# Fewer, larger and later loads on SP in a fused linear-attention and feed-forward kernel

## The chip, the core and the metric

The kernel runs on one core of one Trainium2 chip. The metric is the device time of one execution in microseconds. Engines: PE (TensorE, matrix products), PEld (its weight loads), DVE (VectorE), ACT (ScalarE), POOL (GpSimd), and SP, which computes nothing: it issues DMAs, in the order of the program. POOL issues four DMAs too, for a weight. A DMA lands some microseconds after it was issued.

## The reference

Four batches of eight heads, 768 positions, head dimension 64: a recurrence with a decay for each head, then a feed-forward layer with a squared ReLU over the 3072 x 512 result. All inputs and the output are float32.

```python
gamma = 1.0 - 2.0 ** (-5.0 - np.arange(H, dtype=np.float32))
for t in range(S):
    state = gamma * state + einsum('bhd,bhe->bhde', k[:, :, t], v[:, :, t])
    y[:, :, t] = (1 / sqrt(D)) * einsum('bhd,bhde->bhe', q[:, :, t], state)
x = y.transpose(0, 2, 1, 3).reshape(B * S, H * D)      # 3072 x 512
h = np.maximum(x @ w_in, 0.0)                          # w_in 512 x 2048
out = (h * h) @ w_out                                  # w_out 2048 x 512
```

## The kernel before

**Chunks.** The sequence of each batch is cut in 6 chunks of 128 positions, 24 chunks in all (chunk m is chunk m % 6 of batch m // 6). For a chunk the kernel makes scores (q times k, masked), a running state (k times v, summed over the chunks of a batch) and outputs (scores times v, plus state times q). The decay is put into q and into k or v as a factor, so that the state is a plain sum. The outputs of two chunks make a block of 256 rows for the feed-forward layer (the first block has four chunks).

**Chunks 8 to 23** go like this (`attend2`): POOL casts k to bf16 with two heads side by side (`cast_k2`, L658, two instructions); SP transposes the result by DMA (`transpose_k2`, L681, from ks_bdp to kT); DVE scales v (`scale_v2`, L667, one instruction over all heads) and POOL copies it (L675, two instructions); for each second chunk DVE scales q (L366) and SP transposes it by DMA (`dma_transpose_q`, L425). Then PE: the state with the first half of the chunk's positions (`state2`, L724; it reads the cast k and the scaled v), the scores (`scores2`, L697; it reads kT and qT), the state with the second half, the outputs (L746 and L753).

**Chunk 4** is done in an older way: DVE scales k (`scale_k`, L366 into ks), PE transposes it (L412).

**Loads.** q comes in one DMA for two chunks (`load_q`, 512 KB, L105). From chunk 8 on, k and v come through `batch_loads` (L147): one DMA for each head, so 8 DMAs cover `size` chunks; all 8 must land before v of the first of these chunks can be scaled, and 4 of them (the even heads, the odd heads) for each of the two casts of k. `(8, "k")` covers chunks 8 to 11 with size 4, `(12, ...)` chunks 12 to 17 and `(18, ...)` chunks 18 to 23 with size 3, in two rounds each. A row that a DMA moves is 64 numbers, 256 bytes.

**The order is written by hand.** Between any two pieces of the feed-forward work on PE lies a numbered *place*, and `put(place, what, ...)` hangs a step on it; within one place steps go in the order in which they were put. A place is about 0.87 us of PE work from place 49 on (eight products of 128x256). Each engine runs its own instructions in this order and waits where a semaphore says so; SP knows no places as times, so that it runs ahead or falls behind. `attend2` puts the steps of chunk m from its output place d: k cast at d-18, q scaled at d-19 and d-18, q transposed at d-16, k transposed at d-13, v scaled at d-9, first state at d-6, scores at d-5, second state at d-3. For m = 12, d is 86, and 8 places more for each next chunk; chunks 8 to 11 have places of their own (`ahead`). `load_q(m)` is at d-33. The two stores of a block come in the second and third piece of the next block's first product (L886 and L888). For chunk 10: q transposed at 54, k transposed at 57. For chunk 11: v of chunk 10 scaled and k of chunk 11 cast at 60, k transposed at 63.

The first weight, w_in, is loaded and cast in quarters (`cast_w`, "V" on DVE, "G" on POOL); the quarters of w_out are loaded by POOL, the first at place 10. The sums of `seven_products` use seven products where a product of two-by-two blocks has eight; they add work on DVE that PE reads.

Of the kernel before, what the change touches and what calls it, by code (L numbers as in the profile page):

```python
# [28 lines left out]
def kernel(  # L29
# [97 lines left out]
    def stage_tile(size):  # L127
        t = stage.tile([P, 2 * NCH * NPAIR * D], FP32, name="stage")
        return t[:, 0:size]
# [3 lines left out]
    def batch_loads(m, name, size):  # L133


        b, i = chunks[m]
        src, to = (k, raw_k) if name == "k" else (v, raw_v)
        t = kept_tiles.pop((m, name), None)
        if t is None:
            t = stage_tile(2 * NCH * NPAIR * D)  # L140
        t = t.rearrange("s (p w d) -> s p w d", p=NPAIR, d=D)
        for j in range(NCH - i):
            to[m + j] = t[:, :, 2 * j : 2 * j + 2].rearrange("s p u d -> s u p d")
        for w in range(0, NCH - i, size):
            for hh, rows in enumerate(halves):
                for p in range(NPAIR):
                    nc.sync.dma_start(  # L147
                        t[rows, p, 2 * w : 2 * (w + size)],
                        src[b, 2 * p + hh, (i + w) * C : (i + w + size) * C].rearrange(
                            "(w s) d -> s w d", s=64  # L150
                        ),
                    )
                    yield
# [1061 lines left out]
    def put(place, what, *args):  # L1215
        parts.setdefault(place, []).append((what, args))
# [4 lines left out]
    def attend(m, q_at, qturn_at, k_at, v_at, turn_at, scores_at, state_at, outputs_at):  # L1221
        if m % 2 == 0:
            for r, place in enumerate(q_at):
                put(place, scale_q, m, r)
            put(qturn_at, transpose_q, m)
        put(k_at, scale_k, m)
        put(v_at, cast_v, m)
        put(turn_at, transpose_k, m, m == 4)
        for half, place in enumerate(scores_at):
            put(place, scores, m, half)  # L1230
        put(state_at, state, m)
        put(outputs_at, outputs, m)
# [16 lines left out]
    put(10, load_w_out, 0)  # L1249
    put(11, cast_w, "in", 3, (0,), ".VGV")  # L1250
    put(12, cast_w, "in", 3, (1,), "GVGV")
    attend(4, (8, 9), 11, 11, 11, 12, (14, 15), 15, 17)
    put(13, load_w_out, 1)
    put(17, load_q, 6)
    attend(5, None, None, 17, 18, 18, (20, 21), 21, 23)
# [44 lines left out]
    for m, d in zip(range(PACK_FROM, NCHUNK), done):  # L1300
# [4 lines left out]
    places = {  # L1305
        (8, "k"): [23, 23, 24, 24, 25, 32, 32, 33],
        (8, "v"): [33, 33, 34, 34, 35, 35, 36, 36],
        (12, "k"): [49, 50, 51, 52, 53, 54, 55, 56] + [74 + j for j in range(8)],
        (12, "v"): [58, 59, 60, 61, 62, 64, 65, 66] + [82 + j for j in range(8)],
        (18, "k"): [92 + 4 * j // 3 for j in range(8)] + [117 + 4 * j // 3 for j in range(8)],  # L1310
        (18, "v"): [103 + 4 * j // 3 for j in range(8)] + [128 + 4 * j // 3 for j in range(8)],
    }
    for (m, name), at_places in places.items():
        loads = batch_loads(m, name, 4 if m == 8 else 3)
        for place in at_places:
            put(place, next, loads)

# [53 lines left out]
```

## Time and profile before

| what | value |
|---|---|
| runs shown | 210.73, 212.37, 212.43 us; median 212.37 |
| profiled execution | 213.31 us, of it a span of 211.1 us |
| granted TensorE clock | 0.989 |
| PE busy | 195.8 us (93%) |
| PEld, DVE, ACT, POOL busy | 165.0, 153.5, 136.0, 69.4 us |
| loads of 96 KB by L147 | 32 for k, 32 for v; median 3.4 and 3.3 us to landing |
| loads of 128 KB by L147 | 8 for k, 8 for v; median 4.9 and 5.7 us to landing |
| DMA transposes of k, of q | 16, median 3.5 us to landing; 8, median 4.8 us |
| stores of 256 KB | 23, median 2.6 us to landing |

The span is the time from the program's first to its last instruction; times of single rows count from its start. In rows in order of time the first number is the start and the second the duration, xN says how many instructions are merged, and the bracket holds the idle time of the engine before it and what ended it. For SP a row's duration is the issue alone, not the transfer. In rows of one source line, the three numbers are the shortest, the median and the longest duration in ns.

### The profile page before, as it was taken

Reading aid. Unit: us, or ns where it says so; the run is one execution under the profiler, and the core shown is the slowest. Engines: PE = TensorE matmul, PEld = TensorE weight load, DVE = VectorE, ACT = ScalarE, POOL = GpSimd, SP = SyncE. Lnnn points to the kernel's source line nnn. Section 1 sums busy time; section 2 is a strip of 40 time slices with the busy share of each in tenths; the row PEclk is TensorE's granted clock in tenths of the full one; section 3 lists DMA queues with packets and bytes.
Section 4 is the critical chain, followed back from the end, with each engine's and each line's share of the span. In section 5 each row is a group of like instructions: output and inputs, shape, how many; then the busy total and the mean of one; then the engine's idle time right before and its main releaser. Section 6 shows DMA issues by size and latency. Waiting matters only on the chain.

```text
span 211.1 us, 5854 instructions
## 1 busy us (share of the span) xinstructions
PE 195.8 (93%) x2369; PEld 165.0 (78%) x2373; DVE 153.5 (73%) x305; ACT 136.0 (64%) x276; POOL 69.4 (33%) x134
## 2 busy tenths in 40 slices
PE   5789979999999999699999699799999999999993
PEld 1467634876988998688989599699989999998883
DVE  4777899498897777489597489389688697564374
ACT  8365876577853677492795495584795785783730
POOL 5332458903130254062236044142244236010000
PEclk9889999999999999999999999999999999999999
DMA  6999999998999969689669889999969750500202
GB/s 170 290 317 383 285 252 237 200 198 199 236 174 186 241 180 218 136 207 235 145 183 216 167 197 214 138 266 162 172 175 233 154 101 13 143 0 0 102 0 99
DMA packets 93258, 38.12 MB, mean 181 GB/s; under 512 B 68528, under 2 KB 89264, under 8 KB 93232
## 3 DMA queue, kind: packets, MB, share of 16 engines
q1 hardware_dynamic: 91120, 35.66, 78.1%
q0 software_dynamic: 2112, 2.10, 6.1%
q8 instruction: 18, 0.29, 0.7%
q14 instruction: 8, 0.07, 0.1%
HBM read 27.26 MB, written 6.29 MB: 159 GB/s over the span
## 4 chain that ended last, share of the span: by engine, by line
PE 69%; DMA 15%; DVE 6%; ACT 4%; issue 3%; POOL 1%; SPq 1%; DVEq 0%
PE psf L803 29%; PE psf L837 12%; PE tp L837 8%; PE psf L1096 6%; DMA kT<-ks_bdp 6%; DMA stage<-in_moe_w_in_dram 4%; DMA w_out_bf<-in_moe_w_out_dram 4%; PE psf L1002 3%; DMA qn<-in_q_dram 2%; PE st L697 2%; PE y L753 1%; PE y L746 1%; PE c_ps L724 1%; DVE h L774 1%; ACT h L812 1%
## 5 line engine op out<-in xcount | busy, mean ns | idle before, releaser
L803 PE MATMUL psf<-xt,w_in_bf 128*128 128x256 bf16 (+2 forms) x878 | 92.1, 259 | 0.1
L803 PEld LDWEIGHTS <-w_in_bf 128*128 128x128 bf16 x880 | 70.9, 98 | 10.6 <-issue 0.4
L812 ACT ACTIVATE h<-psf 128x512 bf16<-128x512 f32 x96 | 56.3, 595 | 23.9 <-PE psf L803 23.4
L774 DVE TENSOR_TENSOR h<-h 128x512 bf16<-128x512 bf16 x72 | 32.8, 472 | 15.3 <-ACT h L812 15.0
L658 POOL CAST ks_bdp<-stage 64x512 bf16<-64x512 f32 x32 | 24.0, 750 | 48.3 <-issue 24.5
L675 POOL COPY v_bd<-v 64x512 bf16<-64x512 bf16 x32 | 20.6, 642 | 40.9 <-DVE v L667 29.2
L837 PEld LDWEIGHTS <-h 128*128 128x128 bf16 x288 | 26.3, 98 | 3.6 <-DVE h L774 0.7
L833 DVE TENSOR_TENSOR osb<-psf,u 128x256 f32<-128x256 f32 x34 | 13.7, 422 | 17.4 <-ACT u L878 10.1
L366 DVE TENSOR_TENSOR qs<-qn,qf 128x512 bf16<-128x512 f32 x22 | 17.4, 795 | 1.0 <-DMA qn<-in_q_dram 1.0
L760 ACT ACTIVATE xt<-y 128x512 bf16<-128x512 f32 x16 | 12.0, 748 | 8.8 <-PE y L753 8.8
L704 DVE TENSOR_TENSOR pt<-st,cmask 128x512 bf16<-128x512 f32 x16 | 11.0, 687 | 6.1 <-PE st L697 5.9
L837 PEld LDWEIGHTS <-k_bd 128*128 128x128 bf16 x144 | 13.8, 98 | 1.6
L772 ACT ACTIVATE h<-h 128x512 bf16<-128x512 bf16 x24 | 14.6, 627 | 0.5
L733 ACT ACTIVATE s_bd<-c_ps 64x256 bf16<-64x256 f32 x29 | 10.6, 366 | 3.4 <-PE c_ps L724 3.3
L667 DVE TENSOR_TENSOR v<-stage,kf 128x512 bf16<-128x512 f32 x16 | 12.6, 786 | 0.0
L837 PE MATMUL tp<-w_out_bf,h 128*128 128x256 bf16 x72 | 11.2, 273 | 0.2 <-DVE h L774 0.2
L734 ACT ACTIVATE s_bd<-c_ps 64x256 bf16<-64x256 f32 x29 | 11.0, 379 | 0.4
L697 PE MATMUL st<-qT,kT 128*128 128x64 bf16 x128 | 6.4, 193 | 5.1 <-DMA kT<-ks_bdp 5.1
L833 DVE TENSOR_TENSOR k_bd<-h 128x512 bf16<-128x512 bf16 x18 | 10.7, 597 | 0.3
L837 PE MATMUL psf<-w_sum,h 128*128 128x256 bf16 x72 | 10.8, 273 | 0.0
L697 PEld LDWEIGHTS <-kT 128*128 128x128 bf16 x128 | 5.6, 98 | 6.1 <-DMA kT<-ks_bdp 5.9
L837 PE MATMUL psf<-w_sum,k_bd 128*128 128x256 bf16 x80 | 10.4, 273 | 0.0
(144 smaller groups left out, 310.1 us busy)
## 6 DMA issues: line engine op xcount, KB each, us to landing
qn<-in_q_dram SPq DMA_DIRECT2D x12, 512.0 KB, 5.6
out_dram<-osb SPq DMA_DIRECT2D x23, 256.0 KB, 2.6
stage<-in_k_dram SPq DMA_DIRECT2D x32, 96.0 KB, 3.4
stage<-in_v_dram SPq DMA_DIRECT2D x32, 96.0 KB, 3.3
stage<-in_moe_w_in_dram SPq DMA_DIRECT2D x4, 512.0 KB, 6.9
stage<-in_moe_w_in_dram SPq DMA_DIRECT2D x2, 1024.0 KB, 10.9
w_out_bf<-in_moe_w_out_dram POOLq DMA_DIRECT2D x4, 512.0 KB, 10.6
kn<-in_k_dram SPq DMA_DIRECT2D x2, 512.0 KB, 6.4
```

Of the source, the lines that this page charges most:

```text
L366: engine.tensor_tensor(out=out, in0=by, in1=table[:, :, None].to_broadcast([P, H, D]), op=ALU.mult)
L658: nc.gpsimd.tensor_copy(ks[rows, :, hh, :].rearrange("s (u p) d -> s u p d", u=2), kn[rows])
L667: nc.vector.tensor_tensor(out=v2.rearrange("s (u p) d -> s u p d", u=2), in0=vn, in1=kf2[:, i, :, :, None].to_broadcast([P, 2, NPAIR, D]), ...
L675: nc.gpsimd.tensor_copy(v_bd[rows, :, hh, :], v2[rows])
L697: nc.tensor.matmul(st[:, c, :], lhsT=kT[:, c, :], rhs=half_of(a["qT"], p, u), start=True, stop=True,)
L772: nc.scalar.activation(hv, hv, AF.Square)
L774: nc.vector.tensor_mul(hv, hv, hv)
L803: nc.tensor.matmul(hp, lhsT=w_in_bf[g][:, cb, fq * 128 : (fq + 1) * 128], rhs=xts[tb][:, cb, cols], start=(cb == 0), stop=(cb == NCB - 1),)
L812: nc.scalar.activation(hv, hp[:], AF.Relu)
L833: nc.vector.tensor_tensor(out=out, in0=in0, in1=in1, op=op)
L837: nc.tensor.matmul(to, lhsT=left[:, j], rhs=right(j) if callable(right) else right[:, j], start=(start and j == 0), stop=(stop and j == NF ...
L1096: nc.tensor.matmul(to[:], lhsT=left(j), rhs=right(j), start=(start and j == 0), stop=(j == NFB // 2 - 1), skip_group_check=True,)
```

## The change

- Chunk 4's k is scaled on DVE at place 10, not 11: ahead of the weight casts of place 11.
- Batch 12's first round (chunks 12 to 14): the k loads go from places 49 to 56 to places 58 to 65, the v loads from 58 to 66 to places 66 to 73. So they come after chunk 10's transposes (54 and 57) in SP's order; five k loads stand ahead of chunk 11's k transpose (63), all but the last v load ahead of chunk 12's (73). Before, all eight k loads stood ahead of chunk 10's k transpose and 13 of the 16 ahead of chunk 11's.
- Batch 18 (chunks 18 to 23): one round of 8 loads of 192 KB for k and one for v, where there were two rounds of 8 loads of 96 KB for each. k at places 94, 96, ... 108 (before: 92 to 101, and 117 to 126), v at 109, 111, ... 123 (before: 103 to 112, and 128 to 137). The v of chunk 18 is scaled at place 125; its k is transposed at 121.

The bytes that are moved, the rows of 256 bytes and the arithmetic stay as they are.

```diff
-    attend(4, (8, 9), 11, 11, 11, 12, (14, 15), 15, 17)
+    attend(4, (8, 9), 11, 10, 11, 12, (14, 15), 15, 17)
...
-        (12, "k"): [49, 50, 51, 52, 53, 54, 55, 56] + [74 + j for j in range(8)],
-        (12, "v"): [58, 59, 60, 61, 62, 64, 65, 66] + [82 + j for j in range(8)],
-        (18, "k"): [92 + 4 * j // 3 for j in range(8)] + [117 + 4 * j // 3 for j in range(8)],
-        (18, "v"): [103 + 4 * j // 3 for j in range(8)] + [128 + 4 * j // 3 for j in range(8)],
+        (12, "k"): [58 + j for j in range(8)] + [74 + j for j in range(8)],
+        (12, "v"): [66 + j for j in range(8)] + [82 + j for j in range(8)],
+        (18, "k"): [94 + 2 * j for j in range(8)],
+        (18, "v"): [109 + 2 * j for j in range(8)],
     }
     for (m, name), at_places in places.items():
-        loads = batch_loads(m, name, 4 if m == 8 else 3)
+        loads = batch_loads(m, name, {8: 4, 12: 3, 18: 6}[m])
         for place in at_places:
             put(place, next, loads)
```

## The prediction

> **What bounds the kernel now.** I read the page first: PE 93% busy, and the chain of waits gives 6% to DMA kT<-ks_bdp. The rows in order of time for PE then show where it stands still, apart from the start:
>
> ```profile
> 86.16 0.41 PE L697 MATMUL st<-qT,kT 128*128 128x64 bf16 x8 [1.86 <-DMA kT<-ks_bdp]
> 118.33 0.41 PE L697 MATMUL st<-qT,kT 128*128 128x64 bf16 x8 [1.73 <-DMA kT<-ks_bdp]
> 134.95 0.41 PE L697 MATMUL st<-qT,kT 128*128 128x64 bf16 x8 [1.47 <-DMA kT<-ks_bdp]
> ```
>
> These are the scores of chunks 10, 14 and 16, each waiting for its k transposed by DMA: 5.06 us in all. From 135 to 205 us the windows show PE busy for 5.00 of every 5 us, so only what comes earlier can move the end. Why the transposes are late is in the rows of SP and of POOL:
>
> ```profile
> 80.50 2.03 SPq L147 DMA_DIRECT2D stage<-in_k_dram  x3
> 82.64 1.27 SPq L681 DMA_TRANSPOSE kT<-ks_bdp  x1
> 83.96 3.30 SPq L147 DMA_DIRECT2D stage<-in_v_dram  x5
> 87.36 2.37 SPq L681 DMA_TRANSPOSE kT<-ks_bdp  x1
> ...
> 93.45 2.22 SPq L425 DMA_TRANSPOSE qT<-qs  x1
> 95.78 1.38 SPq L681 DMA_TRANSPOSE kT<-ks_bdp  x1
> 97.20 5.58 SPq L147 DMA_DIRECT2D stage<-in_k_dram  x7
> ```
> ```profile
> 76.16 1.36 POOL L658 CAST ks_bdp<-stage 64x512 bf16<-64x512 f32 x2
> 82.05 1.28 POOL L675 COPY v_bd<-v 64x512 bf16<-64x512 bf16 x2 [4.53 <-PE psf L837]
> 83.39 1.28 POOL L658 CAST ks_bdp<-stage 64x512 bf16<-64x512 f32 x2
> ```
>
> Chunk 10's k was cast at 77.52, its transpose issued at 82.64: SP issues one DMA right behind another and is late by its own work. A load of 96 KB takes it 0.62 us and 0.05 to the next (the five from 83.96 to 87.36: 0.68 each); I use 0.67.
>
> **Part 1, chunk 4's k scaled a place sooner.** DVE does ks (0.68 us) ahead of two squares and two weight casts. PE's wait for it goes:
>
> ```profile
> 31.47 0.40 PE L412 MATMUL tp<-ident,ks 128*128 128x128 bf16 x4 [1.09 <-DVE ks L366]
> ...
> 36.34 1.04 PE L1002 MATMUL psf<-w_out_bf,h 128*128 128x512 bf16 x4 [0.35 <-DMA w_out_bf<-in_moe_w_out_dram]
> ```
>
> But the next wait is fixed: w_out lands at 36.30, issued by POOL at 28.69 after a cast that waited for w_in, none of it touched. The 1.09 us move into that wait. The casts end 0.7 later, near 31.5, where the products that read them began at 31.70. Value 0; were w_out not the cover, it would be -1.1, and +0.7 if PE caught the casts.
>
> **Part 2, batch 12's first loads behind chunk 10's transposes.** Between 70.81 and chunk 10's k transpose SP keeps four stores (some 2.1 us), a q load (0.45 to 1.90) and chunk 10's q transpose (1.38 to 2.68): done by 77.5 at the latest, as the cast ends. It issues at 77.6 and lands 3.47 later (as before) at 81.1; PE wants it at 86.16 - 1.86 = 84.30. **-1.86**, with 3.2 us to spare.
>
> What is late next: the loads were moved, not removed. SP issues five (78.9 to 82.3), then meets chunk 11's transpose, which must wait for POOL's second cast, 83.39 + 1.28 = 84.67. That cast stands behind the v_bd copies of 82.05, which wait for DVE's v and not for SP. So SP, with nothing to spare, waits 2.0 us at chunk 10's and 2.4 us at chunk 11's, and the loads behind it wait too. Chunk 11's transpose goes at 84.73, 2.63 sooner than before, but eight loads that were ahead of it (8 x 0.67 = 5.36) are now behind. Before, the stretch from its issue to the end of chunk 12's transpose took 97.20 - 87.36 = 9.84 us; now seven more loads lie in that: 9.84 + 4.69 = 14.53, and the eighth v load of batch 12 goes out at 99.26 (before: 91.10). At the page's 3.3 us it lands at 102.6. All eight are needed by one DVE operation, and PE needs its result:
>
> ```profile
> 98.88 0.69 DVE L667 TENSOR_TENSOR v<-stage,kf 128x512 bf16<-128x512 f32 x1
> ```
> ```profile
> 100.59 0.28 PE L724 MATMUL c_ps<-v,ks_bdp 128*128 128x64 bf16 x4
> ```
>
> Chunk 12's v is scaled from 102.6 to 103.3. PE, 1.86 early, would be at chunk 12's state (L724) at 98.73 and stands for **+4.6**. Queued behind the waiting operation on DVE: three adds to osb and chunk 12's mask; PE is held by the same load, so they cost nothing more. Bounds by the rows: landing 2.5 to 5.1 us, and issues of 0.9 us a q or k transpose less where the queue has drained: +1.7 to +6.4. I take the middle because the before run spent its 9.84 us on these very DMAs. Net at chunk 12: +2.7.
>
> Chunk 14: its transpose (issued at 114.88) came 27.52 us after chunk 11's; now 84.73 + 27.52 + 5.36 = 117.61, landing 3.41 later at 121.0. PE arrives at 118.33 - 1.73 + 2.7 = 119.3 and waits 1.7 where it waited 1.73: **0.0**.
>
> **Part 3, the last batch in eight issues a tensor in place of sixteen.** 192 KB in one issue is not in the trace. The nearest rows are one line's issues of 128 KB (49 to 64 us) and of 96 KB (later):
>
> ```profile
> L147 SPq DMA_DIRECT2D stage<-in_v_dram x8: 595/672/1675, 56.5 to 62.7; - x8
> ```
> ```profile
> L147 SPq DMA_DIRECT2D stage<-in_v_dram x32: 601/621/2412, 84.0 to 161.7; - x32
> ```
>
> A third more rows of 256 bytes cost nothing at the minimum (595 against 601 ns) and 8% at the median. I take 0.62 us; the upper end is 1.24, in proportion to size. Between the two, 192 KB per 0.67 us would be 293 GB/s, and no slice after the fifth moved over 266: 0.74 where several follow each other. The Trainium skill (Perfetto Trace Analysis, What "DMA-bound" means) says that a solid sequencer track is descriptor generation, paid per descriptor. By that rule an issue with twice the descriptors takes 1.24 us and the merge saves SP nothing; the rows of 595 and 601 ns speak against it.
>
> Between the transposes of chunks 14 and 16 SP has 7 loads for 11: 129.85 - 114.88 = 14.97, less 4 x 0.67 is 12.29, so chunk 16's goes at 129.90 and lands by 135.0 even at its old 5.05. PE wants it at 134.95 - 1.47 + 2.7 = 136.2: **-1.47**, net +1.25.
>
> The last v load sits at place 123, behind chunk 18's transposes. SP must now wait for chunk 18's scaled q (DVE, 140.12 + 1.25 = 141.4), then 1.83 for its transpose, a load, the k transpose (1.27 to 1.93), a load: issue at 145.9 to 146.6. Landing: 3.3 us by the 96 KB row to 5.1 by the 128 KB rows; nearer the first, as SP has stopped crowding, 3.4. DVE's v for chunk 18 then ends at 150.0 to 150.7; PE wants it at 148.82 + 1.25 = 150.07. **+0.5** (0 to 2.3). The loads that leave 139 to 162 us free SP where PE waits for nothing: 0.
>
> **Sum:** 0 - 1.86 + 4.6 + 0.0 - 1.47 + 0.5 = +1.8 us. The profiled execution took 213.31 (span 211.1, 2.2 around it), 0.9 over the median: 215.1 on its scale, **214.1** on the median of 212.37. One per cent, 2.1 us, is about what a measurement of this kernel tells from no change.
>
> **Rivals.** *SP catches up (faster).* Its 4.4 us of waiting let the transfers drain, so that behind them a k transpose costs 1.27 for 2.37, the q transpose 1.25 for 2.22, and loads land in 2.5 us. The last v load goes at 97.2, lands at 99.7; PE waits 1.7 at chunk 12, net -0.1. If the slow issues at 98.54 and 108.19 vanish too (0.95 and 1.29), chunk 14's goes at 113.3, lands at 116.7 against 116.5: net -1.6 there and -3.1 after chunk 16. Half way to it is -0.7. For: 2.5 us landings between 90 and 106. Against: slow issues come every 11 us (87.36, 98.54, 108.19, 119.60, 131.84) whatever stands in the queue, and the q transpose is still near a 512 KB load. 209.3 to 211.7. It decides from the point where the last v load lands before 98.
>
> *The larger loads clog (slower).* At 0.95 us each chunk 16's transpose goes at 131.6 and costs PE 0.4; to chunk 18's are 8 x 0.95 in place of 9 x 0.67, so 146.75; the last v load goes at 149.7, lands at 153.1, and PE stands 3.3 us at chunk 18's state: +5.0, 217.4. At 1.29 (in proportion to size) chunk 16's goes at 133.6 and costs 1.7, the last v load goes at 154.7 and PE stands 7.1 us at chunk 18's state: +10, 222. That is what the Trainium skill's rule above would give. The rival decides from 0.8 us an issue. For: transfers of 5 us behind 128 KB loads. Against: the issue rows.
>
> *Nothing changes:* the transposes wait for something else than SP's place. The unbroken rows of SP speak against it. 212.4.
>
> **Chances.** Forecast 0.48 (+0.6 to +3.5, 213.0 to 215.9; half of it over 1%), catching up 0.30 (0.20 over 1% faster, 0.10 within), clogging 0.17, nothing 0.05. Faster 0.20, within 1% 0.24 + 0.10 + 0.05 = 0.39, slower 0.24 + 0.17 = 0.41. The range, 210.0 to 218.0, leaves out the lower third of catching up and the upper half of clogging.
>
> **What would show it.** Right: no wait at L697 near 84; a new wait of 3 to 5 us at L724 near 98 with DVE L667 waiting for stage<-in_v_dram; some 1.7 at chunk 14's L697; none at chunk 16's; SP idle before the L681 issues of 77.6 and 84.7. Wrong: the last v load of batch 12 issued before 96 (the SP sum), or in_k and in_v issues of 192 KB over 0.8 us (the size of part 3).

## The result, and the profile after

The changed kernel is slower: median 222.64 us of 6 runs (220.40 to 224.58), against 211.92 us of 6 runs before (210.73 to 212.43); the ratio is 1.0495, 95% interval 1.0431 to 1.0560. The profiled execution took 223.16 us with a span of 221.2 us, 10.1 more than the span before. The forecast was 214.1 us, the range 210.0 to 218.0. Some executions run 1.5% or more above the fastest of their kernel; the ratios leave these out, the medians and ranges do not.

The page of the changed kernel:

```profile
span 221.2 us, 5835 instructions
...
PE 200.3 (91%) x2373; PEld 167.2 (76%) x2373; DVE 153.0 (69%) x305; ACT 136.0 (61%) x276; POOL 69.4 (31%) x134
...
PEclk9999999999999999998899999999599999999999
...
L667 DVE TENSOR_TENSOR v<-stage,kf 128x512 bf16<-128x512 f32 x16 | 12.6, 787 | 13.3 <-DMA stage<-in_v_dram 13.3
...
L724 PE MATMUL c_ps<-v,ks_bdp 128*128 128x64 bf16 x116 | 8.3, 196 | 11.5 <-DVE v L667 11.5
...
stage<-in_k_dram SPq DMA_DIRECT2D x8, 192.0 KB, 4.9
```

The idle time in the L724 row is new: PE stands for 11.5 us ahead of the state, for a v that DVE (13.3 us idle in the L667 row) could not scale because its loads had not landed. The k loads of 192 KB land after 4.9 us in the median and the v loads after 4.0; I had taken 3.4 for the v load that mattered. The PEclk line falls in two places, near 105 and near 158 us. The rows in order of time for PE show the waits one by one:

```profile
36.19 1.04 PE L1002 MATMUL psf<-w_out_bf,h 128*128 128x512 bf16 x4 [1.08 <-DMA w_out_bf<-in_moe_w_out_dram]
...
83.98 0.40 PE L697 MATMUL st<-qT,kT 128*128 128x64 bf16 x8
...
103.27 0.37 PE L724 MATMUL c_ps<-v,ks_bdp 128*128 128x64 bf16 x4 [4.71 <-DVE v L667]
...
121.14 0.41 PE L697 MATMUL st<-qT,kT 128*128 128x64 bf16 x8 [0.27 <-DMA kT<-ks_bdp]
...
136.13 0.40 PE L697 MATMUL st<-qT,kT 128*128 128x64 bf16 x8
...
156.90 0.40 PE L724 MATMUL c_ps<-v,ks_bdp 128*128 128x64 bf16 x4 [6.75 <-DVE v L667]
```

From top to bottom: part 1's 1.09 us moved into the wait for w_out; chunk 10's scores without a wait; the new wait at chunk 12's state; chunk 14's 0.27; chunk 16's scores without a wait; and 6.75 us at chunk 18's state, where 0.5 was forecast. The kernel before had no wait there (no bracket in its row):

```profile
148.82 0.28 PE L724 MATMUL c_ps<-v,ks_bdp 128*128 128x64 bf16 x4
```

The rows of SP say why the first came as forecast and the last did not:

```profile
77.39 1.23 SPq L681 DMA_TRANSPOSE kT<-ks_bdp  x1
78.68 3.48 SPq L147 DMA_DIRECT2D stage<-in_k_dram  x5
84.53 1.45 SPq L681 DMA_TRANSPOSE kT<-ks_bdp  x1
...
97.17 2.11 SPq L681 DMA_TRANSPOSE kT<-ks_bdp  x1
99.32 0.60 SPq L147 DMA_DIRECT2D stage<-in_v_dram  x1
...
133.79 3.10 SPq L147 DMA_DIRECT2D stage<-in_v_dram  x2
137.00 2.69 SPq L681 DMA_TRANSPOSE kT<-ks_bdp  x1
...
142.46 0.43 SPq L105 DMA_DIRECT2D qn<-in_q_dram  x1
142.94 0.71 SPq L147 DMA_DIRECT2D stage<-in_v_dram  x1
143.75 5.18 SPq L425 DMA_TRANSPOSE qT<-qs  x1
148.98 0.61 SPq L147 DMA_DIRECT2D stage<-in_v_dram  x1
149.70 1.30 SPq L681 DMA_TRANSPOSE kT<-ks_bdp  x1
151.04 1.38 SPq L147 DMA_DIRECT2D stage<-in_v_dram  x2
```

SP waits ahead of 77.39 and 84.53 and gives out the last v load of batch 12's first round at 99.32 (forecast 77.6, 84.73, 99.26). Later a load of 192 KB still costs it 0.6 us, but single issues stand: 2.10 of the 3.10 us at 133.79 are one load, and chunk 18's q transpose holds SP for 5.18 us. The last v load of batch 18 goes out at 151.75 (forecast 145.9 to 146.6) and lands at 155.84.

### The profile page after: what moved, and what is told of

Same layout as the page of the kernel before. It is cut to its first block, busy times and chain, and to the rows that moved or that the text cites. A ratio compares the mean times of both kernels' runs of the same rounds, so it can differ in the third digit from the quotient of the medians.

```text
span 221.2 us, 5835 instructions
## 1 busy us (share of the span) xinstructions
PE 200.3 (91%) x2373; PEld 167.2 (76%) x2373; DVE 153.0 (69%) x305; ACT 136.0 (61%) x276; POOL 69.4 (31%) x134
## 4 chain that ended last, share of the span: by engine, by line
PE 66%; DMA 14%; DVE 7%; SPq 4%; ACT 3%; issue 3%; POOL 0%; DVEq 0%
PE psf L803 30%; PE psf L837 10%; PE tp L837 6%; PE psf L1096 6%; DMA stage<-in_moe_w_in_dram 4%; DMA w_out_bf<-in_moe_w_out_dram 3%; DMA stage<-in_v_dram 3%; PE psf L1002 3%; DMA kn<-in_k_dram 2%; DMA kT<-ks_bdp 2%; PE st L697 2%; DVE k_bd L833 2%; SPq L681 2%; PE c_ps L724 1%; DVE h L774 1%
## 5 line engine op out<-in xcount | busy, mean ns | idle before, releaser
L803 PE MATMUL psf<-xt,w_in_bf 128*128 128x256 bf16 (+2 forms) x880 | 95.6, 264 | 0.4 <-DVE w_in_bf L336 0.3
L803 PEld LDWEIGHTS <-w_in_bf 128*128 128x128 bf16 x880 | 72.2, 99 | 12.4 <-DVE w_in_bf L336 0.7
L667 DVE TENSOR_TENSOR v<-stage,kf 128x512 bf16<-128x512 f32 x16 | 12.6, 787 | 13.3 <-DMA stage<-in_v_dram 13.3
L724 PE MATMUL c_ps<-v,ks_bdp 128*128 128x64 bf16 x116 | 8.3, 196 | 11.5 <-DVE v L667 11.5
L724 PEld LDWEIGHTS <-ks_bdp 128*128 128x128 bf16 x116 | 7.2, 99 | 12.5 <-DVE v L667 7.0
```

Of the source, the lines that this page charges most:

```text
L667: nc.vector.tensor_tensor(out=v2.rearrange("s (u p) d -> s u p d", u=2), in0=vn, in1=kf2[:, i, :, :, None].to_broadcast([P, 2, NPAIR, D]), ...
L724: nc.tensor.matmul(c[:, p, :], lhsT=a["ks"][:, u * NPAIR + p], rhs=a["v2"][:, u * NPAIR + p, :], start=(i == 0 and u == 0 and p == 0), sto ...
L803: nc.tensor.matmul(hp, lhsT=w_in_bf[g][:, cb, fq * 128 : (fq + 1) * 128], rhs=xts[tb][:, cb, cols], start=(cb == 0), stop=(cb == NCB - 1),)
```

## The experiments

Theories of the 6.75 us at chunk 18's state. *Transfers* (T): the larger loads bring the bytes of all six chunks ahead of chunk 18's transposes and of its own last v load; SP's issues and the landings are held up behind them. *Place* (P): the loads stand too late in SP's order, whatever their size. *Inherited* (I): what went wrong at chunk 12 left SP and PE out of step. The first four kernels ran together beside the kernel before (median 211.80 us there).

**part1: chunk 4's k a place sooner, alone**

```diff
-    attend(4, (8, 9), 11, 11, 11, 12, (14, 15), 15, 17)
+    attend(4, (8, 9), 11, 10, 11, 12, (14, 15), 15, 17)
```

> Chunk 4's k at place 10, nothing else changed. All theories: PE's wait of 1.09 us at L412 goes and the wait at L1002 grows from 0.35 to about 1.1 us; w_out lands at 36.2 to 36.4 as before; 211.9 us, within 0.5.

Measured: 214.86 us, but from a profiled execution of 210.89 and three runs of 214.81 to 215.55, which settles nothing. So the same kernel ran again.

> Chunk 4's k at place 10 alone, once more: the first three timed runs were 214.8 to 215.6 us where the profiled run was 210.89 and the sum says 0. If those three were chance: 211 to 212.5. If the order of DVE's work at 28 to 32 us costs time in most executions: 214 to 215.5, and a profile of such an execution shows a wait before 40 us that the kernel before does not have.

Measured: 213.24 us median of 12 runs beside 212.86 of the kernel before, ratio 1.0007 (0.9968 to 1.0046). Part 1 costs and brings nothing that this measurement can tell, as forecast; the three runs of the first time are not borne out. The way was another than expected: in both profiles PE does not wait at L1002, for w_out landed 6.7 and 6.6 us after its issue (7.6 in the kernel before), and PE took it at 35.78 and 35.69 us instead of 36.34. So the landing of w_out is not fixed. Chunk 10's wait for kT, which part 1 does not touch, was 0.39 and 1.06 us in these two profiles and 1.86 in the kernel before: the 1.86 that part 2 was to win is the figure of one execution.

**part2: batch 12's first loads later, alone**

```diff
-        (12, "k"): [49, 50, 51, 52, 53, 54, 55, 56] + [74 + j for j in range(8)],
-        (12, "v"): [58, 59, 60, 61, 62, 64, 65, 66] + [82 + j for j in range(8)],
+        (12, "k"): [58 + j for j in range(8)] + [74 + j for j in range(8)],
+        (12, "v"): [66 + j for j in range(8)] + [82 + j for j in range(8)],
```

> Batch 12's first loads moved, nothing else. My sum: no wait at chunk 10, 4.7 us at chunk 12's state (L724) behind DVE's v, a wait under 1 us at chunk 14 and 0 to 1 at chunk 16 (there the old eleven loads of 96 KB stand ahead of its transpose), none at chunk 18: +1.3 to +2.8 us, 213.2 to 214.7. Rival, that this move is the cost of the whole change (SP never recovers): chunk 18's state waits over 3 us here too, 219 or more.

Measured: 215.26 us, ratio 1.0173 (1.0107 to 1.0239), more than expected. PE waits 4.17 us at chunk 12's state (102.81), takes 1.27 us more than before for the products behind it (the clock, below) and, in the rows of PE, still waits at chunk 16's scores, 1.42 us where 0 to 1 was expected:

```profile
119.97 0.41 PE L697 MATMUL st<-qT,kT 128*128 128x64 bf16 x8
...
136.53 0.41 PE L697 MATMUL st<-qT,kT 128*128 128x64 bf16 x8 [1.42 <-DMA kT<-ks_bdp]
```

Chunk 14's wait (119.97) is gone. There is none at chunk 18's state, so the rival by which this move costs it all is out.

**part3: the last batch in loads of 192 KB, alone**

```diff
-        (18, "k"): [92 + 4 * j // 3 for j in range(8)] + [117 + 4 * j // 3 for j in range(8)],
-        (18, "v"): [103 + 4 * j // 3 for j in range(8)] + [128 + 4 * j // 3 for j in range(8)],
+        (18, "k"): [94 + 2 * j for j in range(8)],
+        (18, "v"): [109 + 2 * j for j in range(8)],
...
-        loads = batch_loads(m, name, 4 if m == 8 else 3)
+        loads = batch_loads(m, name, {8: 4, 12: 3, 18: 6}[m])
```

> The last batch in loads of 192 KB at places 94 to 123, nothing else. Theory T (the DMA engines fall behind the larger loads: issues stay at 0.62 us, landings go to 6 or 7 us, chunk 18's q transpose and last v load come late): waits at chunks 10 and 14 as before, none at chunk 16, 5 to 7.5 us at chunk 18's state: +5 to +8 us, 217 to 220. Theory I (inherited: chunk 18 is late because the move of batch 12 had put SP 2 us behind): at most 1 us at chunk 18, 210.4 to 212.

Measured: 219.53 us, ratio 1.0352 (1.0297 to 1.0406). The rows of PE:

```profile
134.65 0.41 PE L697 MATMUL st<-qT,kT 128*128 128x64 bf16 x8 [1.49 <-DMA kT<-ks_bdp]
...
153.59 0.29 PE L724 MATMUL c_ps<-v,ks_bdp 128*128 128x64 bf16 x4 [4.91 <-DVE v L667]
```

The wait at chunk 18 is there without part 2, so I falls; it is just under the 5 to 7.5 us that T gave. That chunk 16's wait stays I had not expected: its transpose went out at 128.12, sooner than before, and landed 6.48 us later. Parts 2 and 3 alone add 1.7% and 3.5%, together 5.2% where the whole change adds 4.95% (4.3 to 5.6).

**half: the new places, but 96 KB a load**

```diff
-        (18, "k"): [94 + 2 * j for j in range(8)],
-        (18, "v"): [109 + 2 * j for j in range(8)],
+        (18, "k"): [94 + 2 * j for j in range(8)] + [126 + j for j in range(8)],
+        (18, "v"): [109 + 2 * j for j in range(8)] + [134 + j for j in range(8)],
...
-        loads = batch_loads(m, name, {8: 4, 12: 3, 18: 6}[m])
+        loads = batch_loads(m, name, 4 if m == 8 else 3)
```

This diff is against the changed kernel, as are the next two.

> The changed kernel, but the last batch's first round at the same sixteen places in loads of 96 KB (chunks 18 to 20), and a second round for chunks 21 to 23 at places 126 to 141. Theory T: the same number of issues with half the bytes lands in 3 to 4.5 us, chunk 18's state waits 0 to 1 us: 213 to 215. Theory P (the place alone: the last v load stands behind chunk 18's transposes at place 123 and is too late whatever its size): over 4 us at chunk 18's state, 218 to 222.

Measured: 214.54 us, ratio 1.0124 (1.0061 to 1.0187). No wait at chunk 18's state. The rows of SP there:

```profile
140.94 1.27 SPq L425 DMA_TRANSPOSE qT<-qs  x1
142.25 0.67 SPq L147 DMA_DIRECT2D stage<-in_v_dram  x1
143.03 1.28 SPq L681 DMA_TRANSPOSE kT<-ks_bdp  x1
144.35 1.78 SPq L147 DMA_DIRECT2D stage<-in_v_dram  x2
```

Same order, same places, half the bytes a load: the q transpose takes 1.27 us for 5.18, and the last v load goes out at 145.5 (what I had forecast for the whole change, within 0.4) and lands at 148.7, just in time: v is scaled by 149.72, and PE takes it at 149.78. P falls as a cause by itself. What half still costs is part 2's: 3.89 us at chunk 12's state. But the place is not innocent: in the kernel before the eighth v load of that round was the last of these six,

```profile
131.19 4.80 SPq L147 DMA_DIRECT2D stage<-in_v_dram  x6
```

gone out at 135.4 and landed at 138.5, 10.3 us ahead of chunk 18's state, where half has 1.1 and no wait. So 9 us of cover were there; the places used them up, and the bytes came on top: 6.2 us more at the last issue and 0.9 at the landing.

The next three ran beside a kernel before of 212.86 us median.

**q_later: chunk 20's q load behind chunk 18's transposes**

```diff
-            put(d - 33, load_q, m)
+            put(124 if m == 20 else d - 33, load_q, m)
```

> The changed kernel with the q load of chunks 20 and 21 (512 KB) at place 124, behind the last v load, where it stood at 117 ahead of chunk 18's transposes. Theory T (the DMA engines have more bytes ahead of chunk 18's v than they can move in time): chunk 18's q transpose issues in 1.3 to 3 us where it took 5.18, the last v load lands some 3 us sooner, chunk 18's state waits 3 to 4.5 us where it waited 6.75: 217.5 to 220. Rival (the larger loads themselves hold SP, whatever else is queued): as changed, 221.5 to 223.5.

Measured: 219.82 us, ratio 1.0316 (1.0239 to 1.0392). The rows of SP, then PE's wait:

```profile
141.83 1.39 SPq L425 DMA_TRANSPOSE qT<-qs  x1
143.26 0.62 SPq L147 DMA_DIRECT2D stage<-in_v_dram  x1
143.99 2.90 SPq L681 DMA_TRANSPOSE kT<-ks_bdp  x1
146.93 1.30 SPq L147 DMA_DIRECT2D stage<-in_v_dram  x2
```
```profile
153.01 0.40 PE L724 MATMUL c_ps<-v,ks_bdp 128*128 128x64 bf16 x4 [3.36 <-DVE v L667]
```

With the 512 KB taken out of the queue ahead of it, the q transpose issues in 1.39 us; the k transpose behind it takes 2.90 in its turn. Chunk 18's state comes 3.9 us sooner and its wait is halved, not gone. So the long issue of the q transpose is the queue's doing, as T says, and it is not the larger loads alone that hold SP.

**v_first: the v loads at places 109 to 116, one a place**

```diff
-        (18, "v"): [109 + 2 * j for j in range(8)],
+        (18, "v"): [109 + j for j in range(8)],
```

> The changed kernel with the last batch's v loads at places 109 to 116, one a place, so that all stand ahead of that q load and of chunk 18's transposes. Theory T: the same bytes are ahead of chunk 18's k transpose, so the wait moves rather than goes: chunk 18's state waits 0 to 1.5 us, its scores (L697) 1.5 to 4 us: 216 to 219. Theory P' (only the order of the last two v loads is at fault): no wait at either, 213 to 214.5.

Measured: 217.21 us, ratio 1.0186 (1.0120 to 1.0253). Its profiled execution took 221.2 us, 4 us over the median, and is read for the place of the waits only: 1.52 us at chunk 16's scores and 1.40 at chunk 18's, whose k transposes were now behind the v loads, and 1.55 still at chunk 18's state. P' wanted none and is out. The wait spreads from one tensor to several with the order; part of it goes.

**pool_stores: the kernel before, with the stores issued by POOL**

```diff
-                        nc.sync.dma_start(out[r0 + C : r0 + 2 * C], ob[:])
+                        nc.gpsimd.dma_start(out[r0 + C : r0 + 2 * C], ob[:])
...
-                        nc.sync.dma_start(out[r0 : r0 + C], oa[:])
+                        nc.gpsimd.dma_start(out[r0 : r0 + C], oa[:])
...
-        nc.sync.dma_start(out[r0 : r0 + C], (e.oa, e.ob)[which][:])
+        nc.gpsimd.dma_start(out[r0 : r0 + C], (e.oa, e.ob)[which][:])
```

This goes at the wait that the change was aimed at by another way: SP gets fewer issues, and no load moves.

> The kernel before, with the output stores of L886, L888 and L1071 issued by POOL in place of SP; no load is moved. If the waits at chunks 10, 14 and 16 are SP's count of issues: SP has four issues (2.1 us) less ahead of chunk 10's transpose and two (1.0 us) less in each block, so the wait at chunk 10 goes and those at chunks 14 and 16 shrink to 0 to 1.5 together: 207.5 to 210.5. Rival: POOL's issues hold its casts, or the bytes and not the issues make the transposes late: 211 to 214.

Measured: 210.29 us of 4 runs, ratio 0.981 (0.9726 to 0.9895); in the profiled execution (208.16 us) no scores waited for kT at all. With so few runs it was repeated, on another chip (kernel before there 213.79 us):

> The kernel before with the stores issued by POOL, once more in more rounds, since the interval of the first was 1.7% wide. If the gain is real, 206.5 to 210.5 us, ratio 0.972 to 0.990, and no wait of more than 0.3 us at L697 for chunks 10, 14 and 16; if the first result was chance, as part1's first was, the ratio comes out at 0.99 to 1.00.

Measured: 212.03 us of 12 runs, ratio 0.9924 (0.9887 to 0.9960). The interval leaves out 1, so a gain stands, nearer to 0.8% than to 2%; by the bands set beforehand the ratio lies in that of chance (0.99 to 1.00). The test by the waits was missed too: in this profiled execution (212.70 us) scores wait for kT again, as the view of waits has it:

```profile
PE st L697 <- DMA kT<-ks_bdp: 3.7, 4, 1.8
```

That is 3.7 us in four waits, where the kernel before had 5.06 in three. So these waits vary between executions of one kernel, and that the gain comes from them is not shown. The kernel is faster than the one before and the changed one, by less than its first four runs had it.

**after_pool: the whole change, with the stores on POOL**

The edit is that of pool_stores, made to the changed kernel.

> The whole change with the stores of the later blocks (L886, L888, L1071) issued by POOL, as in pool_stores. Two theories of the +10. Transfers (T): the 192 KB loads bring all six chunks' bytes ahead of chunk 18's transposes, so the landings of 4 to 7 us stay; SP gains about two stores of 0.65 us ahead of the last v load of batch 12 (issue near 98, PE's wait at chunk 12's state 3 to 3.5 where it was 4.71) and about as much ahead of chunk 18's (issue 148 to 150 for 151.75, wait 4 to 5.5 for 6.75). Time 217 to 220, 7 to 10 above pool_stores alone. Issue (S): what was short is SP's time alone, and the stores taken off it leave room for the change: both waits fall under 1 us, time 208 to 212.5, the same as pool_stores alone within 1%.

Measured, beside the last: 222.09 us, ratio 1.0371 (1.0300 to 1.0442), 10.1 us over the same stores without the change. The rows of PE:

```profile
102.73 0.28 PE L724 MATMUL c_ps<-v,ks_bdp 128*128 128x64 bf16 x4 [3.85 <-DVE v L667]
...
154.52 0.29 PE L724 MATMUL c_ps<-v,ks_bdp 128*128 128x64 bf16 x4 [4.53 <-DVE v L667]
```

The time came out above both expectations, but S, by which SP's own time was all that was short, is out: it wanted both waits under 1 us. Fewer issues take about 2 us from the later wait (4.53 for 6.75, one profile each) and leave the rest.

## Why the prediction was wrong, step by step

**Part 1, 0:** right in the size. In the changed kernel the wait at L412 went, and 1.08 us stand ahead of w_out; alone it measures 1.0007. That the wait for w_out took up all of it was partly the luck of this execution: in both profiles of part 1 alone w_out landed 0.9 to 1.0 us sooner after its issue, and there was no wait for it.

**Part 2, chunk 10 and chunk 12:** right, term by term. Chunk 10's transpose went out at 77.39 and landed with 2.5 us to spare; the scores come 2.18 us sooner (forecast 1.86). The last v load went at 99.32, and chunk 12's state is 2.68 us late (forecast +2.7). "SP catches up" falls here: it needed that load to land before 98, and it landed at 102.35.

**Chunks 14 and 16:** right in the sum, by another way at chunk 14. PE came to its scores 1.6 us later than forecast, because it had run slowly after chunk 12 (below), and so waited 0.27 instead of 1.7; the transposed k let it go on at 121.14, and its landing had been forecast for 121.0. After chunk 14 the kernel was 2.81 us late, after chunk 16's scores 1.18 (forecast +1.25).

**Part 3, chunk 18, +0.5 (0 to 2.3):** this step failed. "in_k and in_v issues of 192 KB over 0.8 us" is what I said would show it wrong, and the issue was sized well: the view of line 147 from 105 to 155 us of the changed kernel, in which 8 of the 16 v loads and 8 of the 9 k loads are of 192 KB, has

```profile
L147 SPq DMA_DIRECT2D stage<-in_v_dram x16: 604/618/2100, 106.7 to 151.8; - x16
L147 SPq DMA_DIRECT2D stage<-in_k_dram x9: 604/622/787, 106.0 to 133.0; - x9
```

a median of 0.62 us over 96 and 192 KB alike. The Trainium skill (Perfetto Trace Analysis, What "DMA-bound" means) has a solid sequencer track as descriptor generation, with a cost per descriptor. From it the prediction had worked out 1.24 us for twice the descriptors; these rows do not show that. What failed is that I took SP's issues for the whole price of a load. I had bounded what is in the queue behind the loads by 96 KB rows: a q transpose of 1.83 us and a landing of 3.4, "as SP has stopped crowding". It had not: SP reached the q transpose at 143.75, 2.35 us after the forecast's 141.4 (the scaled q was there at 141.29), stood in it 3.35 us longer than that row, and the landing took 4.09. These three make 6.4 us, and the wait was 6.25 longer than forecast. The windows from 110 to 155 us, of the kernel before, of half and of the changed kernel, have in their last two columns the DMA share (the time of the packets over 16 engines) and the rate in GB/s:

```profile
110.00:155.00 45.00, 41.80 (x505) 37.48 (x504) 32.71 (x62) 29.07 (x63) 15.76 (x22) 1.00 1.05 194
```
```profile
110.00:155.00 45.00, 44.56 (x542) 39.94 (x541) 35.19 (x67) 31.69 (x67) 16.72 (x24) 1.00 0.98 188
```
```profile
110.00:155.00 45.00, 39.88 (x487) 35.66 (x485) 31.38 (x57) 28.49 (x60) 15.04 (x21) 0.99 1.25 196
```

With the larger loads packets took longer and hardly more was moved. That SP's issue had paced the 96 KB loads before is my reading of this, not shown. The 16 loads hold 16 x 96 KB = 1.57 MB more ahead of chunk 18's last v load; against half, that load was issued 6.2 us later. At the 196 GB/s that were moved these bytes would take 8.0 us, an estimate that leaves nothing for gaps.

The rival "larger loads clog" had the place, the sign and, at its far end, the size (+10), but not the mechanism: it wanted issues of 0.95 to 1.29 us. Chunk 16 shows the difference: no wait there, where the far end of the rival had 1.7 (by the 5.05 us to landing that it takes at its near end it would be 2.5, which leaves its total as it is).

**A term that the sum did not have:** what a long wait does to PE afterwards. From chunk 18's state to chunk 19's scores lie the same 116 products in the records, without a gap, before and after: 148.82 to 158.93, 10.11 us, and 156.90 to 169.09, 12.19 us. The windows of the changed kernel show it in the column of the granted clock, the third from the right:

```profile
150.00:155.00 5.00, 0.15 (x2) 0.00 (x0) 0.00 (x0) 0.44 (x2) 0.00 (x0) 0.94 1.23 205
155.00:160.00 5.00, 3.10 (x24) 2.43 (x25) 2.22 (x5) 1.35 (x3) 1.22 (x2) 0.50 0.43 96
160.00:165.00 5.00, 5.00 (x45) 4.24 (x44) 2.86 (x6) 3.13 (x7) 1.30 (x2) 0.88 0.25 67
165.00:170.00 5.00, 5.00 (x66) 4.49 (x65) 4.56 (x11) 4.11 (x9) 1.30 (x2) 1.00 0.93 198
```

Half the clock from 155 to 160, then 0.88, then full. The kernel before has it full where it makes these products:

```profile
150.00:155.00 5.00, 5.00 (x57) 4.51 (x54) 3.74 (x8) 3.94 (x9) 1.30 (x2) 1.00 0.92 216
155.00:160.00 5.00, 5.00 (x66) 4.49 (x64) 4.55 (x10) 4.08 (x9) 1.30 (x2) 1.00 0.72 163
```

That is 2.08 us more. At chunk 12 the same stretch took 11.70 us for 10.11; chunk 14's wait absorbed that 1.59.

The shifts against the kernel before add up: chunk 16's scores +1.18, chunk 18's state +8.08, chunk 19's scores +10.16, the end +10.1. Of the 8.3 us that the forecast of +1.8 missed, 6.25 are the wait at chunk 18 and 2.08 the clock behind it.

## What to carry to other kernels

Price a merged load twice: by the issue, which hardly grows with its size, and by the bytes that it puts into the queue ahead of whatever is needed next, transposes on the same queue included; merging took eight issues a tensor off SP and, at the same places, lost eight microseconds (222.64 us against the 214.54 of half). When the place of loads is moved later, write down how far ahead of need the last of them lands (here 9 us of cover became none) before anything that can slow that queue is added. And price a long wait of PE at more than its length: in this kernel those of 3.36 us and more cost 1.3 to 2.7 us on top, those of up to 2.18 us nothing.

## What the hardware showed that was not expected

**The clock after a wait.** Over all profiles but that of v_first the 116 products behind chunk 12's or chunk 18's state took 10.11 us in every case without a wait ahead (10.31 with the stores on POOL). After waits of 3.36, 3.89, 4.17, 4.53, 4.71, 4.91 and 6.75 us they took 12.81, 11.75, 11.38, 12.51, 11.70, 11.77 and 12.19: 1.3 to 2.7 us more, with no tie to the wait's length. With the stores on POOL they took 11.96 and 11.97 after 3.85 and 4.53. After waits of up to 2.18 us (chunk 14 in the second profile of part 1) the granted clock stayed at 1.00. The Trainium skill (TensorE: Matmul & The Clock Gate, Part 1: The HAM clock gate) says that the array falls to half its clock after an idle window of about 3.4 us and comes back after about as long of steady work, in windows that run free of the program. The trace agrees on the half, 0.50 granted, and by that page the loss would be an estimated 1.7 us, inside the 1.3 to 2.7 measured.

The granted clock, read every 0.25 us, shows why the wait's length says little. In these nine cases it stands at 0.50 for 3.4 us (six) or twice that, 6.8 us (three), as windows of that length would have it, and what is lost is about half of the time of it in which PE works. It fell 2.2 to 5.1 us after PE had stopped, in four cases only when PE was at work again. The wait of 3.36 us (q_later) had the worst place: the clock fell at 151.8, 2.2 us after PE had stopped, and came back at 158.6, so that PE ran at half for 5.6 us from 153.01 on; behind the 6.75 us of the changed kernel it was 4.3 us, from 156.90 to 161.2. So here the clock fell after less idle time than the 3.4 us that the page gives, and the measurement decides.

**An issue that grows with the queue.** Chunk 18's q transpose took SP 5.18 us behind a q load of 512 KB and a v load of 192 KB whose transfers were still to come (they landed 7.07 and 7.23 us after issue), 3.33 us in part3, and 1.27 to 1.39 us where the queue was shorter (half) or the q load gone from it (q_later). What in the queue holds the issue, the number of its descriptors or its bytes, these runs do not tell apart; nor did any run move the same bytes in 96 KB loads at these places, which would part the size of a load from the sum of the bytes.
